# A ring of four PSUM banks for attention and feed-forward, three steps of a head pair in another place, and overwritten products of the identity ahead of P's transposes

## The chip, the cores and the metric

The kernel runs on one core of one Trainium2 chip. The metric is the device time of one execution in microseconds (us).

## The reference

```python
scores = (q @ k.transpose(0, 1, 3, 2)) / sqrt(64)      # q, k, v: 8 x 8 x 576 x 64
scores = where(pos_i // 64 >= pos_j // 64, scores, -1e9)  # causal over blocks of 64
scores = scores - max(scores)
attn = exp(scores)
attn = attn / (sum(attn) + 1e-9)
x = (attn @ v).transpose(0, 2, 1, 3).reshape(4608, 512)
h = x @ w_in                                            # 512 x 2048
g = where(h >= 1, h, where(h <= -1, 0, (h + 1) ** 2 / 4))
out = g @ w_out                                         # 2048 x 512
```

Everything is fp32, with 8 batches of 8 heads and 576 tokens of 64 values each.

## The kernel before

Attention goes by pairs of heads: 32 pairs, four to a batch. A pair's work is cut into eight steps by a generator, `attention_steps`, which yields at each step's end. The feed-forward is a second generator, `feed_forward`, with 9 chunks of 512 tokens and 16 blocks of the hidden width in each. `ffn_in` makes one block of the hidden layer with twelve products into the bank `ph` (L770), and from that `t` (L779 on ACT, L780 and L783 on DVE), `gh` (L784) and `gl` (L785). `ffn_out` multiplies `gh` and `gl` by the second weights into four banks `po` (L794, L799), twelve products again. From step 36 on (pair 4's middle) each attention step is followed by one step of the feed-forward. Pair 31 is the last, and the rest of the feed-forward runs alone behind it. In between, both weights are converted in pieces (`prepare_weights`, lines L161 to L185) up to about pair 7, some 276 us from the start.

Precision comes from splitting an operand into a high and a low part in the type fp32r, each in a product of its own; so q and k go as `qa`, `qb`, `ka`, `kb`, x as `xh` and `xl`.

One pair works like this. `turned` and `turned_last` transpose q and k on TensorE (PE) into a bank `ps_qk`, from which ACT and DVE write `qb` and `kb`; `turned_last` does it for the last block of 64 tokens. `scores(j, g)` is head j's group g of query tiles: the products L482 and L485 into a bank `ps_s`, the row maximum (L505, DVE), the exponential with its sum (L509, ACT), the sum's inverse (L491, L492) and the scaling of P (L515, DVE). `scores_last` is the last 64 queries of both heads in one go. `turn(j, g)` and `turn_last` transpose P into a bank `ps_t`; ACT copies it to `pa` or `pb` and DVE subtracts for the low part (L547). The corner, the last 64 keys of the last queries, has a transpose and a bank of its own there, and goes to `pcs`. `attn_v_first` and `attn_v(j)` multiply P by V (L591) into a bank `ps_av`, whose two halves ACT copies (L613) and DVE adds (L614) into x. `store_x` splits x.

Pairs differ by batch. In batches 0 and 1 (`plain`, pairs 0 to 7) P and V stay fp32, and P is transposed at L554; from batch 1 on P is first copied by DMA into an fp32r tile (`as_float32r`). From batch 2 on (`raw`, `far`) q and k come as fp32r from a copy in DRAM, P is transposed at L552, and each step does its turning and its P by V later than in the pairs before. For those the steps are: 0, the old pair's `turn(1, 1)`, `scores(0, 0)`, the old pair's `attn_v_first`; 1, the old pair's `turn(1, 2)`, `scores(0, 1)`, `turned_last`; 2, the old pair's `attn_v(1)` and `store_x`, `scores(0, 2)`; 3, `turn(0, 0)`, `scores_last`; 4, `turn(0, 1)`, `scores(1, 0)`, the next pair's first `turned`; 5, `turn(0, 2)`, `scores(1, 1)`; 6, `turn_last`, `scores(1, 2)`; 7, `turn(1, 0)`, `attn_v(0)`, the next pair's second `turned`.

PSUM has eight banks of 2 KB a partition. Three go round as a ring for all attention banks (`ps_w`, taken through `work_bank`), one is `ph` alone (`ps_h`), and four are `po`; until step 36 `work_bank` lends every other one of its banks from those four. A bank is written again only when its last reader is done.

Instructions are placed in each engine's queue by a scheduler of the framework, in nearly the order of the code, and each engine takes its queue in order. Tile numbers behind a name (`ps_t_8866`) count up through the program and differ between the two kernels.

Of the kernel before, what the change touches and what calls it, by code (L numbers as in the profile page):

```python
# [23 lines left out]
def block_attn_then_ffn(  # L24
# [34 lines left out]
    KA = D + NTL  # L59
    PLAIN = 2  # L60
# [13 lines left out]
    ps_w = ctx.enter_context(tc.tile_pool(name="ps_w", bufs=3, space=bass.MemoryType.PSUM))  # L74
    ps_h = ctx.enter_context(tc.tile_pool(name="ps_h", bufs=1, space=bass.MemoryType.PSUM))
# [4 lines left out]
    def work_bank(name):  # L80

# [173 lines left out]
    class Pair:  # L255
# [238 lines left out]
        def scores(self, j, g):  # L494
# [21 lines left out]
            self.pr[j, g] = as_float32r(pr[:, : cols[-1].stop], self.plain) if self.hop else [pr]  # L516

        def scores_last(self):
# [23 lines left out]
            self.pr["last"] = as_float32r(pr, self.plain) if self.hop else [pr]  # L542

        def split(self, ps, hi, lo=None):
            nc.scalar.copy(hi, ps)
            if lo is not None:
                nc.vector.tensor_tensor(out=lo, in0=ps, in1=hi.bitcast(F32), op=ALU.subtract)  # L547

# [7 lines left out]
        def turn(self, j, g):  # L556
# [15 lines left out]
        def turn_last(self):  # L572
            pr = self.pr.pop("last")
# [34 lines left out]
        def add_halves(self, ps, j, c0):  # L608
# [3 lines left out]
            xtmp = att1.tile([P, G1], F32, tag="xtmp", name="xtmp")  # L612
# [18 lines left out]
        def attn_v_first(self):  # L631
# [3 lines left out]
            for j in range(2):  # L635
                self.weighted(ps[:, j * G0 : (j + 1) * G0], j, self.parts_first(j))
            for j in range(2):
                self.add_halves(ps[:, j * G0 : (j + 1) * G0], j, 0)

        def attn_v(self, j):  # L640
# [4 lines left out]
            self.add_halves(ps, j, G0)  # L645
# [17 lines left out]
    def attention_steps():  # L663
# [10 lines left out]
        for i, cur in enumerate(pairs + [None]):  # L674
# [9 lines left out]
            if far:  # L684
                old.attn_v_first()
# [13 lines left out]
            yield  # L699
            if far:  # L700
                old.attn_v(1)
                old.store_x()
            if not cur:
                return
            if cur.far:
                cur.scores(0, 2)
# [178 lines left out]
```

## Time and profile before

| What | Value |
|---|---|
| Median of three runs | 1268.96 us (1266.4 to 1271.8) |
| Profiled execution, device time | 1269.69 us |
| Its span in the trace | 1267.9 us |
| Mean granted clock of PE | 0.981 |
| PE busy | 1200.1 us, 95% of the span, 6280 instructions |
| PE's weight loads busy | 998.8 us, 79% |
| DVE busy | 887.0 us, 70% |
| ACT busy | 703.2 us, 55% |
| POOL busy | 394.6 us, 31% |
| DMA | 215.43 MB, mean 170 GB/s |
| Chain that ended last | PE 69%, DVE 16%, ACT 6%, issue 5% |

PE is the matmul engine, DVE the vector engine, ACT the scalar engine, POOL GpSimd, SP the engine that issues most transfers. Busy shares are of the whole span. The chain is followed back from the last instruction, at each step to what released it, and its shares say on which engine the end was waiting. The granted clock is the share of TensorE's full speed that the throttle allowed. In the timeline a row has the start, the duration, the engine, the line and the operation, and in brackets the idle time ahead of it with its releaser.

### The profile page before, as it was taken

What the parts mean: (1) busy time and instruction counts of PE and PEld (TensorE: products, weight loads), DVE (VectorE), ACT (ScalarE), POOL (GpSimd) and SP (SyncE); (2) the same over time, 40 slices, a digit from 0 to 9 for tenths busy, and PEclk for the clock granted to TensorE, in tenths of its full rate; (3) what the DMA queues carried; (4) which work ended last, traced back from release to release, by engine and by line L of the source; (5) the groups of instructions that cost most, each with busy time, mean ns of one, the idle gap of its engine ahead of it and who ended that gap; (6) DMA issues with size and microseconds to landing.
All of it is one profiled execution on the core that took longest, in us unless ns stands there. A gap on an engine that the chain in (4) does not pass through costs nothing.

```text
span 1267.9 us, 20253 instructions
## 1 busy us (share of the span) xinstructions
PE 1200.1 (95%) x6280; PEld 998.8 (79%) x6280; DVE 887.0 (70%) x2188; ACT 703.2 (55%) x1827; POOL 394.6 (31%) x430
## 2 busy tenths in 40 slices
PE   5888889899999999999999999999999999999998
PEld 4666667678888888888888888888888888888886
DVE  8898877758777777777777777787777777322222
ACT  5787656646566655665656655566556555222222
POOL 3555655522222222222222222222222222222222
PEclk9888988999999999999999999999999999999999
DMA  5566666667888655555554655465556433422432
GB/s 158 167 176 215 203 228 197 217 198 237 260 273 266 215 162 158 154 175 163 156 162 145 187 157 152 138 189 153 160 154 190 137 128 118 132 87 98 133 100 100
DMA packets 185259, 215.43 MB, mean 170 GB/s; under 512 B 113840, under 2 KB 132272, under 8 KB 184384
## 3 DMA queue, kind: packets, MB, share of 16 engines
q1 hardware_dynamic: 185152, 214.14, 54.9%
q8 instruction: 50, 0.82, 0.3%
q14 instruction: 57, 0.47, 0.1%
HBM read 134.74 MB, written 31.98 MB: 131 GB/s over the span
## 4 chain that ended last, share of the span: by engine, by line
PE 69%; DVE 16%; ACT 6%; issue 5%; DMA 1%; POOL 1%; SPq 1%; ACTq 0%; POOLq 0%; DVEq 0%
PE ph L770 29%; PE po L794 15%; PE po L799 7%; PE ps_av L591 7%; PE ps_s L482 4%; ACT pr L509 3%; PE ps_s L485 3%; DVE t L780 2%; PE ps_t L552 2%; DVE t L783 2%; ACT t L779 2%; DVE pb L547 2%; DVE nm L505 2%; DVE sm L491 1%; DVE pr L515 1%
## 5 line engine op out<-in xcount | busy, mean ns | idle before, releaser
L785 POOL TENSOR_TENSOR gl<-t,gh 128x512 fp32r<-128x512 f32 x144 | 187.5, 1302 | 510.2 <-ACT gh L784 333.2
L794 PE MATMUL po<-wo,gh 128*128 128x512 f32 x1152 | 296.1, 397 | 0.5 <-DMA wo<-wo_split 0.3
L794 PEld LDWEIGHTS po<-wo,gh 128*128 128x128 f32 x1152 | 212.5, 189 | 44.5 <-DMA wo<-wo_split 0.7
L770 PE MATMUL ph<-xh,wih 128*128 128x512 f32 x576 | 232.9, 404 | 1.6 <-DVE t L783 1.6
L770 PE MATMUL ph<-xh,wil 128*128 128x512 f32 x576 | 228.8, 397 | 0.0
L770 PE MATMUL ph<-xl,wih 128*128 128x512 f32 x576 | 227.8, 396 | 0.5 <-DVE xl L627 0.5
L780 DVE SCALAR_TENSOR_TENSOR t<-t 128x512 f32<-128x512 f32 x144 | 101.5, 705 | 168.0 <-ACT t L779 165.2
L779 ACT ACTIVATE t<-ph 128x512 f32<-128x512 f32 x144 | 85.9, 597 | 173.8 <-PE ph L770 173.8
L509 ACT ACTIVATE pr<-ps_s,nm 128x128 f32<-128x128 f32 (+3 forms) x256 | 134.1, 527 | 60.5 <-DVE nm L505 58.4
L784 ACT CAST gh<-t 128x512 fp32r<-128x512 f32 x144 | 89.5, 621 | 120.3 <-DVE t L783 120.0
L799 PE MATMUL po<-wo,gl 128*128 128x512 f32 x576 | 155.6, 392 | 0.0
L482 PE MATMUL ps_s<-ka,qa 68*128 68x288 f32 (+4 forms) x384 | 135.3, 367 | 15.0 <-ACT pr L509 5.4
L379 POOL TENSOR_TENSOR vsr<-vn,vsr 128x256 fp32r<-128x256 f32 (+1 forms) x96 | 55.2, 576 | 246.2 <-ACT vsr L378 244.6
L770 PEld LDWEIGHTS ph<-xh,wil 128*128 128x128 f32 x576 | 109.5, 190 | 23.8
L770 PEld LDWEIGHTS ph<-xh,wih 128*128 128x128 f32 x576 | 109.8, 191 | 21.7 <-DVE t L783 2.3
L799 PEld LDWEIGHTS po<-wo,gl 128*128 128x128 f32 x576 | 108.7, 189 | 23.1
L505 DVE TENSOR_REDUCE nm<-ps_s 128x1 f32<-128x128 f32 (+3 forms) x256 | 118.8, 482 | 10.4 <-PE ps_s L485 9.4
L770 PEld LDWEIGHTS ph<-xl,wih 128*128 128x128 f32 x576 | 109.7, 190 | 20.5 <-DVE xl L627 0.9
L485 PE MATMUL ps_s<-kb,qb 128*128 128x288 f32 (+4 forms) x384 | 121.1, 322 | 0.0
L515 DVE TENSOR_SCALAR pr<-pr,sm 128x128 f32<-128x128 f32 (+3 forms) x256 | 107.3, 440 | 5.4
L783 DVE TENSOR_TENSOR t<-ph,t 128x512 f32<-128x512 f32 x144 | 98.7, 686 | 2.2
L491 DVE TENSOR_SCALAR sm<-sm 128x1 f32<-128x1 f32 (+1 forms) x224 | 52.0, 232 | 68.3 <-ACT pr L509 65.7
(111 smaller groups left out, 1871.4 us busy)
## 6 DMA issues: line engine op xcount, KB each, us to landing
wo<-wo_split SPq DMA_DIRECT2D x144, 512.0 KB, 3.5
prr<-pr SPq DMA_DIRECT2D x96, 192.0 KB, 2.5
prr<-pr SPq DMA_DIRECT2D x72, 256.0 KB, 2.8
out_dram<-ob SPq DMA_DIRECT2D x36, 256.0 KB, 2.9
bits<-in_moe_w_in_dram SPq DMA_DIRECT2D x32, 256.0 KB, 3.5
bits<-in_moe_w_out_dram SPq DMA_DIRECT2D x32, 256.0 KB, 3.0
wo_split<-ws SPq DMA_DIRECT2D x16, 512.0 KB, 2.9
qa<-qb SPq DMA_DIRECT2D x63, 128.0 KB, 2.4
```

The source lines that it names most:

```text
L482: nc.tensor.matmul(ps, qa[:KA, j, c0 : c0 + P], ka[:KA, j, k0 : k0 + n], start=first, stop=False)
L485: nc.tensor.matmul(ps, qb[:, j, c0 : c0 + P], kb[:, j, k0 : k0 + n], start=False, stop=last)
L505: nc.vector.tensor_reduce(out=nm[:, i : i + 1], in_=ps[:, cs], axis=AX.X, op=ALU.max, negate=True)
L509: nc.scalar.activation(pr[:, cs], ps[:, cs], AF.Exp, bias=nm[:, i : i + 1], scale=1.0, accum_out=sm[:, i : i + 1],)
L515: nc.vector.tensor_scalar_mul(pr[:, cs], pr[:, cs], sm[:, i : i + 1])
L770: nc.tensor.matmul(ph, w[:, cc, fs], x[:, cc, xs], start=(cc == 0 and i == 0), stop=(cc == NCC - 1 and i == 2),)
L779: nc.scalar.activation(t_, ph, AF.Relu, bias=0.5, scale=0.5)
L780: nc.vector.scalar_tensor_tensor(out=t_, in0=t_, scalar=1.0, in1=t_, op0=ALU.min, op1=ALU.mult)
L783: nc.vector.tensor_tensor(out=t_, in0=ph, in1=t_, op=ALU.max)
L785: nc.gpsimd.tensor_tensor(out=gl, in0=t_, in1=gh.bitcast(F32), op=ALU.subtract)
L794: nc.tensor.matmul(po[tt], gh[:, ts_], wo[:, w, :], start=(fc == 0 and w == 0), stop=False)
L799: nc.tensor.matmul(po[tt], gl[:, ts_], wo[:, 0, :], start=False, stop=fc == NFC - 1)
```

## The change

It has three parts.

The ring. `ps_h` goes, `ps_w` has four banks, and `ffn_in` takes `ph` through `work_bank` as attention takes its own. `po` keeps four.

The steps of `far` pairs. Step 0 does the old pair's `attn_v(0)` in place of `attn_v_first`, step 1 does `attn_v_first` behind `scores(0, 1)`, and step 2 does `scores(0, 2)` ahead of `attn_v(1)`. Step 7 no longer has `attn_v(0)`. `turned_last` moves from a pair's own step 1 to the end of step 6 of the pair before it. The corner is no longer transposed in step 6 into a bank of its own, but in step 7 into the free columns of `turn(1, 0)`'s bank (`turn_corner`). `add_halves` is given its scratch `xtmp` by the caller, one tile for both calls in `attn_v_first`. `moved` holds what `scores` wrote out before.

The products. In `plain` pairs `turn` and `turn_last` call `dense` ahead of their transposes: two products of the identity with itself, 512 columns each, into the bank that the transposes then overwrite. There are 7 such sets in each of 8 pairs, 112 products of 512 columns in all.

```diff
+    DENSE = 2
...
-    ps_w = ctx.enter_context(tc.tile_pool(name="ps_w", bufs=3, space=bass.MemoryType.PSUM))
-    ps_h = ctx.enter_context(tc.tile_pool(name="ps_h", bufs=1, space=bass.MemoryType.PSUM))
+    ps_w = ctx.enter_context(tc.tile_pool(name="ps_w", bufs=4, space=bass.MemoryType.PSUM))
...
+        def dense(self, ps):
+            part, cols = ident_r.ap
+            moving = bass.AP(tensor=ident_r.tensor, offset=ident_r.offset, ap=[part, [0, 4], cols])
+            for _ in range(DENSE if self.plain else 0):
+                nc.tensor.matmul(ps, ident_r, moving, start=True, stop=True)
...
             ps = work_bank("ps_t")
+            self.dense(ps)
             for c0 in range(0, n, P):
                 self.transposed(ps[:, c0 : c0 + P], pr, c0, P)
+            if self.far and j == 1 and g == 0:
+                self.turn_corner(self.pr.pop(("last",)), ps[:BLK, n : n + P])
...
         def turn_last(self):
...
+            self.dense(ps)
...
-            ps = work_bank("ps_t")
-            self.transposed(ps[:BLK, :P], pr, SM, BLK)
-            self.split(
-                ps[:BLK, :P].rearrange("p (h c) -> p h c", h=2), *(x[:BLK] for x in self.pc)
-            )
+            if not self.far:
+                self.turn_corner(pr, work_bank("ps_t")[:BLK, :P])
...
             if far:
-                old.attn_v_first()
+                old.attn_v(0)
...
                 cur.scores(0, 1)
-                cur.turned_last()
+                if not cur.raw:
+                    cur.turned_last()
...
+            if far:
+                old.attn_v_first()
...
+            cur.scores(0, 2)
             if far:
                 old.attn_v(1)
                 old.store_x()
...
+            if nxt and nxt.raw:
+                nxt.turned_last()
             yield
             if cur.far:
                 cur.turn(1, 0)
-                cur.attn_v(0)
...
-        ph = ps_h.tile([P, 512], F32, tag="ph", name="ph")
+        ph = work_bank("ph")
```

Three places show how instructions move. In these rows a line of PE holds the line of code, the bank written, the operands and, in brackets, what it waits for.

First, PE from step 5 of a far pair to step 1 of the next. Before:

```order
L485 MATMUL ps_s_8830<-kb_107,qb_105 128x384
...
L552 MATMUL ps_t_8866<-ident_r_95,prr_8740 128x128 [waits DMAHW5_49,DVE_49,PE_49]
L552 MATMUL ps_t_8873<-ident_r_95,prr_8742 64x128 [waits DMAHW6_49,DVE_49]
L482 MATMUL ps_s_8877<-ka_106,qa_104 128x512 [waits Activation_49]
L485 MATMUL ps_s_8877<-kb_107,qb_105 128x512
...
L591 MATMUL ps_av_8984<-pa00_8697,vsr0_111 128x256 [waits DVE_49,PE_49]
...
L552 MATMUL ps_t_9011<-ident_r_95,prr_8888 128x128 [waits DMAHW5_49,DVE_49]
L482 MATMUL ps_s_9018<-ka_106,qa_104 128x384 [waits Activation_49]
L485 MATMUL ps_s_9018<-kb_107,qb_105 128x384
L442 MATMUL ps_qk_9031<-ident_r_95,qk_8744 128x128 [waits DVE_49,PE_49]
```

After; the same stretch has these rows, L486 for L485, L566 for L552, L443 for L442, L611 for L591 and L795 for L770:

```order
L486 MATMUL ps_s_9321<-kb_104,qb_102 128x384
...
L566 MATMUL ps_t_9357<-ident_r_92,prr_9231 128x128 [waits DMAHW0_49,DVE_49,PE_49]
L483 MATMUL ps_s_9364<-ka_103,qa_101 128x512 [waits DVE_49]
L486 MATMUL ps_s_9364<-kb_104,qb_102 128x512
L443 MATMUL ps_qk_9377<-ident_r_92,qk_9235 128x128 [waits Activation_49]
...
L566 MATMUL ps_t_9397<-ident_r_92,prr_9289 128x128 [waits DMAHW4_49,DVE_49]
L566 MATMUL ps_t_9397<-ident_r_92,prr_9233 64x128 [waits DMAHW1_49]
L402 MATMUL ps_qk_9406<-ident_r_92,qk_9235 128x128 [waits DVE_49]
L795 MATMUL ph_9417<-xh_94,wih_96 128x512 [waits Activation_49]
...
L611 MATMUL ps_av_9468<-pb0_9192,vsr0_108 128x320 [waits DVE_49,PE_49]
```

The corner (64x128) no longer stands ahead of `scores(1, 2)` in a bank of its own, but behind `turn(1, 0)`'s transposes in theirs. `turned_last` (`ps_qk`, one row of 128 columns) stands right behind `scores(1, 2)`, and no longer behind `scores(0, 1)` of the next pair; and the feed-forward's `ph` and `attn_v(0)`'s first product now wait for ACT and DVE where they take their bank.

Second, DVE over the same steps 6 and 7. Before, whole:

```order
L547 TENSOR_TENSOR pb1_8702<-ps_t_8866,pb0_8701 128x4x2x64 [waits Activation_49]
L783 TENSOR_TENSOR t_8856<-ph_8843,t_8856 128x512 [waits DVE_49]
L547 TENSOR_TENSOR pcs1_110<-ps_t_8873,pcs0_109 64x128 [waits Activation_49]
L505 TENSOR_REDUCE nm_8879<-ps_s_8877 128x1 [waits PE_49]
L491 TENSOR_SCALAR sm_8880<-sm_8880 128x1 [waits Activation_49]
L492 RECIPROCAL sm_8880<-sm_8880 128x1 [waits DVE_49]
L515 TENSOR_SCALAR pr_8878<-pr_8878,sm_8880 128x512 [waits DMAHW6_49,DMAHW5_49,DVE_49]
L547 TENSOR_TENSOR pa11_8700<-ps_t_8902,pa10_8699 128x384 [waits Activation_49]
L614 TENSOR_TENSOR x32_8703<-ps_av_8908,xtmp_8919 64x320 [waits Activation_49,Pool_49]
L389 SCALAR_TENSOR_TENSOR qb_105<-ps_qk_8922,qb_105 64x512 [waits Activation_49]
L395 TENSOR_TENSOR kb_107<-ps_qk_8922,kb_107 64x512 [waits Activation_49]
```

After (L808 is the old L783, L506 the old L505, L390 and L396 the old L389 and L395, L554 the old L547):

```order
L808 TENSOR_TENSOR t_9347<-ph_9334,t_9347 128x512 [waits DVE_49]
L506 TENSOR_REDUCE nm_9366<-ps_s_9364 128x1 [waits PE_49]
L390 SCALAR_TENSOR_TENSOR qb_102<-ps_qk_9377,qb_102 64x2x64 [waits Activation_49]
...
L516 TENSOR_SCALAR pr_9365<-pr_9365,sm_9367 128x512 [waits DMAHW1_49,DMAHW0_49,DVE_49]
L447 TENSOR_SCALAR ka_103<-ps_qk_9377 64x2x64
L554 TENSOR_TENSOR pcs1_107<-ps_t_9397,pcs0_106 64x128 [waits Activation_49]
L390 SCALAR_TENSOR_TENSOR qb_102<-ps_qk_9406,qb_102 64x512 [waits Activation_49]
L554 TENSOR_TENSOR pa11_9191<-ps_t_9397,pa10_9190 128x384 [waits Activation_49]
L396 TENSOR_TENSOR kb_104<-ps_qk_9406,kb_104 64x512 [waits Activation_49]
```

Four small pieces of `turned_last` (64x2x64) have come in behind the row maximum of `scores(1, 2)`, the corner's subtraction (`pcs1`) has moved from ahead of that maximum to behind the scaling of P, and the add of x (L614) has left for a later step.

Third, PE in a `plain` pair, from the products of one `scores` to those of the next. Before:

```order
L482 MATMUL ps_s_934<-ka_106,qa_104 128x384 [waits Activation_49]
L485 MATMUL ps_s_934<-kb_107,qb_105 128x384
L554 MATMUL ps_t_945<-ident_r_95,pr_838 128x128 [waits DVE_49,Activation_49]
L554 MATMUL ps_t_945<-ident_r_95,pr_838 128x128
L554 MATMUL ps_t_945<-ident_r_95,pr_838 128x128 [waits Activation_49]
L554 MATMUL ps_t_945<-ident_r_95,pr_838 128x128
L554 MATMUL ps_t_951<-ident_r_95,pr_838 64x128
L422 MATMUL ps_qk_954<-ident_r_95,ks_888 128x128 [waits Pool_49]
L422 MATMUL ps_qk_954<-ident_r_95,ks_888 128x128 x3
L482 MATMUL ps_s_961<-ka_106,qa_104 128x512 [waits Activation_49]
```

After (L561 is the product of the identity, L568 the old L554):

```order
L483 MATMUL ps_s_965<-ka_103,qa_101 128x384 [waits Activation_49]
L486 MATMUL ps_s_965<-kb_104,qb_102 128x384
L561 MATMUL ps_t_976<-ident_r_92 128x512 [waits PE_49]
L561 MATMUL ps_t_976<-ident_r_92 128x512
L423 MATMUL ps_qk_987<-ident_r_92,ks_917 128x128 [waits Activation_49,Pool_49]
L423 MATMUL ps_qk_987<-ident_r_92,ks_917 128x128 x3
L561 MATMUL ps_t_1005<-ident_r_92 128x512 [waits Activation_49]
L561 MATMUL ps_t_1005<-ident_r_92 128x512
L568 MATMUL ps_t_976<-ident_r_92,pr_865 128x128 [waits DVE_49]
L568 MATMUL ps_t_976<-ident_r_92,pr_865 128x128 x3
L568 MATMUL ps_t_984<-ident_r_92,pr_865 64x128 [waits PE_49]
L483 MATMUL ps_s_994<-ka_103,qa_101 128x512
```

Each bank `ps_t` is first written by two products of 512 columns. Here both sets stand some rows ahead of their transposes; of the 56 sets 42 stand directly ahead of them.

More of the change, by code (lines that the diff above doesn't have):

```diff
@@ L699, in attention_steps @@
             yield
+            if not cur:
+                old.attn_v(1)
+                old.store_x()
+                return
+            if not cur.far:
+                cur.begin()
+            cur.scores(0, 2)
             if far:
@@ L702, in attention_steps @@
                 old.store_x()
[L703 to L706, printed above, removed]
-            else:
-                cur.begin()
-                cur.scores(0, 2)
+            if not cur.far:
                 cur.turn(0, 0)
```

22 lines of the change are left out of this document (15 added, 7 removed).

## The prediction

> **What bounds the kernel now.** I read the totals by stage first, then the clock line of the page, then the chain in the two halves of the first stage, and last, for the long second stage, what TensorE waits for.
>
> ```profile
> PEclk9888988999999999999999999999999999999999
> 0.00:276.00 276.00, 227.38 (x1107) 179.53 (x1108) 221.34 (x601) 181.63 (x526) 140.04 (x177) 0.92 0.63 196
> 276.00:1080.00 804.00, 789.88 (x4369) 668.67 (x4368) 615.80 (x1515) 477.27 (x1228) 210.60 (x220) 1.00 0.58 176
> 1080.00:1267.90 187.90, 182.79 (x807) 150.64 (x805) 49.89 (x73) 44.27 (x74) 43.99 (x34) 0.99 0.33 108
> ```
>
> Columns are the stretch, its length, busy time of PE, PE's weight loads, DVE, ACT and POOL, the granted clock, DMA share and GB/s. The middle stage, pairs 8 to 31 beside the feed-forward, is PE's: 98% busy at full clock. The tail is PE's too and the change leaves it alone. In the first stage, while weights convert, PE is busy 82% and DVE 80%, and the clock is 0.92. Nine stretches there, 44.38 us together, run at half clock; here are the third, the fourth and the sum, and how one product of 512 columns lasts before and after 32.7 us:
>
> ```profile
> 101.02:104.43 3.41, 3.41 (x8) 2.14 (x7) 3.41 (x15) 3.41 (x14) 0.11 (x2) 0.50 0.84 310
> 114.67:118.09 3.42, 3.42 (x10) 2.64 (x9) 3.28 (x8) 1.41 (x5) 1.68 (x2) 0.50 0.55 189
> sum 44.38, PE 40.46 PEld 30.42 DVE 37.72 ACT 26.17 POOL 22.08; mean PE 4.50 PEld 3.38 DVE 4.19 ACT 2.91 POOL 2.45
> L485 PE MATMUL ps_s<-kb,qb 128*128 128x512 f32 x2 | 1.3, 628 | 0.0
> L485 PE MATMUL ps_s<-kb,qb 128*128 128x512 f32 x1 | 0.4, 401 | 0.0
> ```
>
> The last two rows (windows 12.3 to 32.7 and 33 to 49.8) say that the start ran at half clock as well, though its clock column reads 1.00. What a dip costs shows in the chain that ended last, where the same work stands in a dip (first and third row) and out of it:
>
> ```profile
> 101.02 6.56 PE ps_av L591 x20
> 275.16 5.07 PE ps_av L591 x20
> 113.61 4.62 PE ph L770 x12
> 254.83 2.75 PE ph L770 x12
> ```
>
> So a dip of 3.4 us costs 1.5 to 1.9 us where PE is on the chain. It is there only in part:
>
> ```profile
> by line: PE ps_av L591 8.7%; DVE pr L515 8.2%; DVE nm L505 7.6%; DVE work L171 6.9%; PE ps_t L554 6.3%; DVE work L177 5.8%; issue 5.8%; DVE work L174 4.6%; PE ph L770 3.7%; PE ps_s L482 2.9%; DVE nm L529 2.3%; PE ps_s L485 2.1%; DMA ka<-mro
> by line: PE ph L770 15.6%; PE ps_av L591 12.7%; issue 11.5%; POOL work L183 6.7%; PE po L794 5.6%; DVE t L780 3.2%; DMA prs<-pr 3.1%; PE po L799 3.0%; ACT pr L509 2.7%; DMA bits<-in_moe_w_in_dram 2.6%; DMA kn<-in_k_dram 2.2%; DVE t L783 2.2
> ```
>
> From 0 to 145 us (first row) PE's shares add up to 24%, from 145 to 290 us to 37%. DVE carries much of the rest.
>
> The middle stage has two waits of PE that come back in each of its pairs (window 290 to 1080):
>
> ```profile
> PEld ps_qk L442 <- PE ps_s L485: 15.7, 23, 0.7
> PEld ps_s L482 <- ACT pr L509: 10.1, 23, 0.5
> 679.54 0.25 PE L442 MATMUL ps_qk<-ident_r,qk 128*128 128x128 f32 x1 [0.38 <-DVE x L614]
> 711.83 0.41 PE L482 MATMUL ps_s<-ka,qa 68*128 68x384 f32 x1
> 712.08 0.34 PE L485 MATMUL ps_s<-kb,qb 128*128 128x384 f32 x1
> 712.25 0.43 DVE L614 TENSOR_TENSOR x<-ps_av,xtmp 64x256 f32<-64x256 f32 x1
> 712.83 0.25 PE L442 MATMUL ps_qk<-ident_r,qk 128*128 128x128 f32 x1 [0.41 <-DVE x L614]
> ```
>
> First, L442 (`turned_last`) takes the bank of `attn_v_first`, whose last add (L614) ends at 712.68; PE starts at 712.83, 0.75 us after L485. The 384 columns before it need some 0.18 (an estimate from 0.23 us for 512 columns, below), so about 0.57 is lost, 23 times: 13.1 us. Second, `scores(1, 2)` waits for the exponential of `scores(1, 1)`: 10.1 us. Together 23 us of 804.
>
> **The change part by part.** The sum is made against the profiled execution, 1269.69 us with a span of 1267.9; the median of the runs shown, 1268.96, lies 0.7 below it.
>
> *Waits removed.* The corner of the last block no longer takes a bank in step 6, and `turned_last` no longer stands behind `attn_v_first`. Both waits above go: -23. That is one end of this term.
>
> *Waits added.* A step that goes to step 6 brings its work for DVE along, into a stretch where DVE is already late. The rows of one pair:
>
> ```profile
> 731.71 0.51 PE L552 MATMUL ps_t<-ident_r,prr 128*128 128x128 f32 x5
> 732.51 0.50 PE L482 MATMUL ps_s<-ka,qa 68*128 68x512 f32 x1 [0.29 <-ACT pr L509]
> 733.09 2.00 PE L794 MATMUL po<-wo,gh 128*128 128x512 f32 x8
> 735.84 0.37 PE L552 MATMUL ps_t<-ident_r,prr 128*128 128x128 f32 x3
> 734.42 0.68 DVE L783 TENSOR_TENSOR t<-ph,t 128x512 f32<-128x512 f32 x1
> 735.01 0.27 DVE L547 TENSOR_TENSOR pcs<-ps_t,pcs 64x128 fp32r<-64x128 f32 x1
> 735.21 0.67 DVE L505 TENSOR_REDUCE nm<-ps_s 128x1 f32<-128x512 f32 x1
> 735.97 0.69 ACT L509 ACTIVATE pr<-ps_s,nm 128x512 f32<-128x512 f32 x1 [0.22 <-DVE nm L505]
> 681.19 0.28 DVE L389 SCALAR_TENSOR_TENSOR qb<-ps_qk,qb 64x128 fp32r<-64x128 f32 x1
> 737.17 0.49 DVE L515 TENSOR_SCALAR pr<-pr,sm 128x512 f32<-128x512 f32 x1
> 737.57 0.55 DVE L547 TENSOR_TENSOR pa<-ps_t,pa 128x384 fp32r<-128x384 f32 x1
> 738.78 0.68 DVE L389 SCALAR_TENSOR_TENSOR qb<-ps_qk,qb 64x512 fp32r<-64x512 f32 x1 [0.21 <-ACT qb L388]
> 740.11 0.69 DVE L395 TENSOR_TENSOR kb<-ps_qk,kb 64x512 fp32r<-64x512 f32 x1 [0.65 <-ACT kb L394]
> 741.30 1.03 PE L591 MATMUL ps_av<-pa,vsr 128*128 128x256 f32 x8
> ```
>
> I lay the new order on these rows. With the wait gone, PE begins `scores(1, 2)` at 732.0; its two products take 0.58 (732.51 to 733.09), `turned_last` 0.1, the twelve products of `ffn_out` 2.75 (733.09 to 735.84), two sets of four small products 0.6. So the feed-forward's bank `ph` is wanted at 736.0. In the ring of four it is the bank of `scores(1, 2)`, which the exponential frees. The corner's subtraction (L547 of `pcs`) no longer stands ahead of the reduction, so that runs at 735.0 in place of 735.2, the exponential from 735.8 to 736.5, and PE hears of it 0.14 later (the add ended at 712.68, PE started at 712.83): 736.6. New wait: 0.55. Behind it DVE has `turned_last`'s four small pieces (0.28 each), the scaling of P (0.49), the corner (0.27), then `qb` (0.68), P's subtraction (0.55) and `kb` (0.69): 3.8 us, of which one small piece fits in before the exponential ends at 736.5, and with two tiny ones for the sum and its inverse `kb` ends near 740.3. `attn_v(0)` wants that bank 3.6 us after 736.6, at 740.2, and gets it at 740.4: 0.2. The two cost 0.75 in each of 24 pairs, 18 us, and the term is -23 + 18 = -5. It rests on DVE's queue to within some 0.6 us a pair, so it may be from -23 to +9; I take -6, near the sum, because every piece in it has a row.
>
> *The other pieces of the ring.* `ph` and the work banks share four where there were three and one. The closest case on the rows above: `ph` of step 5 is read last by L783, which ends at 735.10, and its bank is wanted by the transposes of step 7 at 735.4. That just fits, so nothing is costed; were L783 half a microsecond later, this would be a third wait. `xtmp` is taken once for two halves, but the second copy still waits for the first add; nothing. `attn_v(1)` behind `scores(0, 2)` delays the write of x by 0.5 us, and its reader comes a step later; nothing, unless that step shrinks.
>
> *The dense products.* 56 sets (7 in each of 8 pairs) of two products of 512 columns: by the row of eight `po` (2.75 us for twelve) 0.23 each at full clock, 25.8 us of PE. They hide where PE waits for P anyway:
>
> ```profile
> L554 PE MATMUL ps_t<-ident_r,pr 128*128 128x128 f32 x96 | 20.4, 339 | 14.8 <-DVE sm L491 7.5 <-DVE pr L515 3.9 <-ACT pr L535 1.6
> L552 PE MATMUL ps_t<-ident_r,vsr 128*128 128x128 f32 x65 | 8.2, 242 | 3.0 <-DMA vsr<-pr 1.4 <-ACT pr L535 1.0 <-DVE xl L627 0.6
> L552 PE MATMUL ps_t<-ident_r,pre 128*64 128x128 f32 x4 | 1.0, 260 | 3.7 <-ACT pr L509 3.0 <-ACT pb L545 0.7
> ```
>
> That is 21.5 us of waiting (up to 276 us), in gaps of up to 3.8. A set fills at most 0.46 of one, so some twenty sets hide, 9 us. Of the other 17 a third would count by PE's share of the chain, all of it if PE were the chain; I take half, +8. Ends: 0 and +25.8.
>
> *The clock.* At most half of 44.4 us, 22, and half of some 20 us at the start come back, -32, if no dip is left; none if all stay. The dips follow stretches in which PE was little busy:
>
> ```profile
> 97.61:101.02 3.41, 1.94 (x17) 1.72 (x16) 3.31 (x9) 2.76 (x8) 2.71 (x4) 1.00 0.83 257
> ```
>
> 1.94 us busy of 3.41, then half clock. Two dense sets there would make it 2.8. I take five of the nine dips as lifted, 20 us of the 44, and the start as a few us shorter: -13. With the price, -5 for this stage. The Trainium skill (TensorE: Matmul & The Clock Gate, Part 1, the table of the two states) has the clock fall after a whole idle window of about 3.4 us. The trace differs: this window was 57% busy. Taken strictly the rule leaves 0.46 us of products in a gap without any effect on the clock, and the sum would be -6 + 8.
>
> Sum: -6 - 5 = -11, so 1258.7 for the profiled execution and 1258 for the median.
>
> **The rivals.** A: PE's new waits do not come, because DVE gets through its queue 0.6 us earlier than I laid it. Then -23 - 5 = -28: 1241. For it: DVE still idles 0.65 us ahead of `kb` in the row at 740.11. Against: 3.8 us of its work stand in line behind the reduction.
>
> B: the dense products do not lift the dips. Then -6 + 8: 1271, no change. For it: a gap of 1.5 us or more is not closed by 0.46. This is what the rule of TensorE: Matmul & The Clock Gate in the Trainium skill would make of it.
>
> C: all dips go, the start's in part: -26 + 8 - 6 = -24: 1245. Against: where PE waits ahead of scores or of the feed-forward, no dense set stands.
>
> D, on the other side: the scheduler issues a dense set as soon as its bank is free, rows ahead of its transposes, while PE has work. Then nothing hides, no gap is filled, and the 25.8 us stand on the path: -6 + 25.8 = +20, 1289; with 12.5 us of them on the path it is slower by 0.5%. Against: in the order most sets stand right ahead of their transposes.
>
> **How the numbers follow.** The median's noise is about 0.5%, 6.3 us: faster is under 1262.6, slower over 1275.3. Chances: the forecast 0.42 (1251 to 1265), A 0.17, B 0.16, C 0.11, D 0.14. Below 1262.6 lie nearly all of A and C and 0.36 of the forecast: 0.63. The same: the rest of the forecast, B but for a little, and a little of D: 0.21. Slower: 0.16. The range 1242 to 1276 leaves out half of A and most of D.
>
> **What the profile after would show.** No wait of `turned_last` on `attn_v_first`, and none of `scores(1, 2)`; in their place one of `ph` on the exponential and of `ps_av` on DVE's `kb`, 0.5 and 0.2 us. A pair's period, 33.3 us now (679.54 to 712.83 at L442), about 33.1. Four dips instead of nine before 276 us, full clock before 32 us, the end of the first stage some 5 us earlier. I am wrong if the new waits are missing or over 1 us, or if the dips stay.

## The result: slower by 0.9%

| | before | changed |
|---|---|---|
| Median | 1267.29 us (1264.21 to 1271.8, 5 runs) | 1278.59 us (1275.79 to 1281.46, 5 runs) |
| Ratio | | 1.0086, 95% interval 1.0068 to 1.0104 |
| Profiled execution, span | 1267.9 us | 1274.8 us |
| Mean granted clock in the profile | 0.981 | 0.992 |

The forecast was 1258, with a range that ended at 1276. The profiled execution of the changed kernel (1276.59) is one of its quicker ones; the five go from clock 0.983 at 1281.46 us to 0.992 at 1275.79.

The totals by stage of the changed kernel, in the columns of the prediction's first totals:

```profile
0.00:276.00 276.00, 233.93 (x1209) 188.09 (x1210) 216.43 (x601) 181.56 (x521) 138.10 (x176) 0.96 0.66 202
276.00:1080.00 804.00, 789.12 (x4339) 664.58 (x4339) 619.75 (x1507) 474.61 (x1228) 210.49 (x220) 1.00 0.57 173
```

The first stage has the clock that was hoped for, 0.96 where it was 0.92, with PE busy 6.6 us longer; the middle stage shows 30 products fewer in the same 804 us. Where a pair's first product of scores starts tells how far each stage got. Pair 8's, the end of the first stage, and the last pair's `scores(1, 2)`, the end of the middle, of before:

```profile
270.46 0.22 PE L482 MATMUL ps_s<-ka,qa 68*128 68x128 f32 x1
1066.05 0.50 PE L482 MATMUL ps_s<-ka,qa 68*128 68x512 f32 x1
```

And of the changed kernel:

```profile
272.92 0.22 PE L483 MATMUL ps_s<-ka,qa 68*128 68x128 f32 x1
1072.96 0.47 PE L483 MATMUL ps_s<-ka,qa 68*128 68x512 f32 x1
```

So the first stage ends 2.5 us later, the middle takes 800.04 in place of 795.59, 4.5 us more, and what follows is the same (201.84 and 201.85 us to the span's end). What PE's weight loads wait for in the middle stage (window 290 to 1080; total, times, longest):

```profile
PEld ph L795 <- ACT pr L510: 8.9, 17, 0.5
PEld ps_qk L443 <- ACT pr L510: 7.9, 23, 0.5
PEld ps_s L483 <- PE ps_t L566: 6.3, 17, 0.4
PEld ps_av L611 <- PE ps_s L486: 4.6, 17, 0.3
```

Both waits of before (25.8 us together) are gone, and `ph` waits for the exponential and `attn_v(0)` (L611) waits, as forecast. The third row is new: `scores(0, 0)`. The second costs PE next to nothing, since at L443 the loads wait while PE is still in the products before. One pair in order of time, PE, ACT and DVE:

```profile
771.14 0.28 PE L443 MATMUL ps_qk<-ident_r,qk 128*128 128x128 f32 x1
774.41 0.69 ACT L510 ACTIVATE pr<-ps_s,nm 128x512 f32<-128x512 f32 x1
775.24 0.50 PE L795 MATMUL ph<-xh,wih 128*128 128x512 f32 x1 [0.38 <-ACT pr L510]
775.51 0.29 DVE L396 TENSOR_TENSOR kb<-ps_qk,kb 64x128 fp32r<-64x128 f32 x1
776.02 0.28 DVE L447 TENSOR_SCALAR qa<-ps_qk 64x128 fp32r<-64x128 f32 x1
776.73 0.29 DVE L447 TENSOR_SCALAR ka<-ps_qk 64x128 fp32r<-64x128 f32 x1
777.06 0.28 DVE L554 TENSOR_TENSOR pcs<-ps_t,pcs 64x128 fp32r<-64x128 f32 x1
777.37 0.48 ACT L552 CAST pa<-ps_t 128x384 fp32r<-128x384 f32 x1 [1.12 <-DVE pcs L554]
777.37 0.69 DVE L390 SCALAR_TENSOR_TENSOR qb<-ps_qk,qb 64x512 fp32r<-64x512 f32 x1
778.09 0.56 DVE L554 TENSOR_TENSOR pa<-ps_t,pa 128x384 fp32r<-128x384 f32 x1
778.10 0.38 PE L566 MATMUL ps_t<-ident_r,prr 128*128 128x128 f32 x3
778.70 0.69 DVE L396 TENSOR_TENSOR kb<-ps_qk,kb 64x512 fp32r<-64x512 f32 x1
778.75 0.30 PE L483 MATMUL ps_s<-ka,qa 68*128 68x128 f32 x1 [0.27 <-PE ps_t L566]
779.54 1.32 PE L611 MATMUL ps_av<-pb,vsr 128*128 128x320 f32 x8
804.93 0.28 PE L443 MATMUL ps_qk<-ident_r,qk 128*128 128x128 f32 x1
```

DVE reads the bank of `turn(1, 0)` last (`pa`, to 778.65), 0.1 us before `scores(0, 0)` starts in it; `kb` ends at 779.39, and `attn_v(0)` starts 0.15 later. For both the views name PE's own work as what came last (the brackets at 778.75, the last row of the list above); that DVE holds them is read from these times, and tested with f2 below. This pair takes 33.79 us (771.14 to 804.93), where the prediction's row had 33.29; over 22 pairs the mean goes from 33.43 to 33.62.

The list of waits alone doesn't give the loss: it holds 25.8 us that went and 19.8 that came (8.9, 6.3 and 4.6), yet the middle stage is 4.5 longer. So PE's lost time was counted over both traces from the start of each product to the start of the next, less 0.23 us for every 512 columns:

| Lost in the middle stage, us | before | changed | difference |
|---|---|---|---|
| `turned_last` and the other turns to `ps_qk` | 15.0 | 1.9 | -13.1 |
| `scores(1, 2)` | 8.8 | 0.8 | -8.0 |
| first product of `ph` | 1.8 | 11.6 | +9.8 |
| `scores(0, 0)` | 0.7 | 7.9 | +7.2 |
| turns to P by V (`attn_v(0)`) | 1.2 | 4.8 | +3.6 |
| `po` behind `po`, at most 0.1 us each | 2.4 | 6.8 | +4.4 |
| turns to P's transposes | 0.4 | 3.4 | +3.0 |
| all else | 46.9 | 44.1 | -2.8 |

The rows add up to +4.1 (the two traces differ by 0.4 in the columns themselves). The first five come to -0.5. The rest of the loss is in small pieces whose cause no run here singles out.

Last, the six half-clock stretches that are left in the first stage, the first of them and their sum, and three of the stretches of 3.41 us ahead of such places:

```profile
24.51:27.92 3.41, 3.02 (x12) 2.14 (x11) 3.27 (x13) 2.59 (x9) 2.19 (x3) 0.50 0.82 265
...
sum 20.49, PE 19.76 PEld 15.07 DVE 15.58 ACT 14.31 POOL 12.02; mean PE 3.29 PEld 2.51 DVE 2.60 ACT 2.38 POOL 2.00
137.15:140.56 3.41, 1.67 (x8) 0.89 (x7) 3.34 (x9) 2.57 (x6) 0.74 (x1) 1.00 0.47 120
41.58:44.99 3.41, 1.75 (x14) 1.38 (x12) 3.07 (x12) 2.43 (x8) 1.61 (x2) 1.00 0.75 184
65.47:68.88 3.41, 0.39 (x2) 0.00 (x0) 3.38 (x11) 1.19 (x4) 1.46 (x2) 1.00 0.02 5
```

20.5 us in place of 44.4, and the start is at half clock until 17.7 us in place of 32.8. The profile's clock, 0.992, is above the mean of the five, 0.989; the kernel before has 0.982 on average over the timed runs beside the experiments. Twice the missing share of the span puts the half-clock time at some 29 us in place of 45 (an estimate, with the few us at the span's end in it), so about 16 us went in an average run and not 24.

### The profile page after: what moved, and what is told of

The parts are those of the page before. It is cut to its first block, busy times and chain, and to the rows that moved or that the text cites. A ratio compares the mean times of both kernels' runs of the same rounds, so it can differ in the third digit from the quotient of the medians.

```text
span 1274.8 us, 20343 instructions
## 1 busy us (share of the span) xinstructions
PE 1212.8 (95%) x6392; PEld 1009.4 (79%) x6392; DVE 889.7 (70%) x2188; ACT 703.4 (55%) x1827; POOL 393.9 (31%) x430
## 4 chain that ended last, share of the span: by engine, by line
PE 61%; DVE 15%; ACT 5%; issue 2%; DMA 2%; POOL 0%; SPq 0%; ACTq 0%; POOLq 0%; DVEq 0%
PE ph L795 24%; PE po L819 14%; PE ps_av L611 8%; PE po L824 7%; PE ps_s L483 3%; PE ps_s L486 3%; ACT pr L510 3%; DVE pb L554 2%; DVE t L805 2%; PE ps_t L566 2%; DVE t L808 2%; DVE pr L516 2%; DVE nm L506 2%; DVE kb L396 1%; DVE sm L492 1%
## 5 line engine op out<-in xcount | busy, mean ns | idle before, releaser
L810 POOL TENSOR_TENSOR gl<-t,gh 128x512 fp32r<-128x512 f32 x144 | 191.9, 1332 | 623.1 <-ACT gh L809 216.6
L795 PE MATMUL ph<-xh,wih 128*128 128x512 f32 x576 | 232.3, 403 | 13.0 <-ACT pr L510 12.7
L819 PEld LDWEIGHTS po<-wo,gh 128*128 128x128 f32 x1152 | 208.1, 188 | 40.0 <-ACT gh L809 0.5
L795 PE MATMUL ph<-xh,wil 128*128 128x512 f32 x576 | 227.0, 394 | 0.0
L795 PE MATMUL ph<-xl,wih 128*128 128x512 f32 x576 | 226.3, 393 | 0.0
L483 PE MATMUL ps_s<-ka,qa 68*128 68x288 f32 (+4 forms) x384 | 129.3, 352 | 10.6 <-PE ps_t L566 4.4
L506 DVE TENSOR_REDUCE nm<-ps_s 128x1 f32<-128x128 f32 (+3 forms) x256 | 119.0, 482 | 28.5 <-PE ps_s L486 28.2
L795 PEld LDWEIGHTS ph<-xh,wih 128*128 128x128 f32 x576 | 109.3, 190 | 35.7 <-ACT pr L510 16.0
L795 PEld LDWEIGHTS ph<-xh,wil 128*128 128x128 f32 x576 | 109.1, 189 | 24.3
L795 PEld LDWEIGHTS ph<-xl,wih 128*128 128x128 f32 x576 | 109.5, 190 | 19.6
L486 PE MATMUL ps_s<-kb,qb 128*128 128x288 f32 (+4 forms) x384 | 119.6, 318 | 0.0
L516 DVE TENSOR_SCALAR pr<-pr,sm 128x128 f32<-128x128 f32 (+3 forms) x256 | 114.6, 468 | 4.7
L808 DVE TENSOR_TENSOR t<-ph,t 128x512 f32<-128x512 f32 x144 | 98.6, 685 | 2.3
L380 POOL TENSOR_TENSOR vsr<-vn,vsr 64x64 fp32r<-64x64 f32 (+1 forms) x96 | 50.8, 530 | 149.3 <-ACT vsr L379 142.4
L566 PEld LDWEIGHTS ps_t<-ident_r,prr 128*128 128x128 f32 x600 | 68.3, 139 | 25.8 <-issue 3.6
```

Of the source, the lines that this page charges most:

```text
L483: nc.tensor.matmul(ps, qa[:KA, j, c0 : c0 + P], ka[:KA, j, k0 : k0 + n], start=first, stop=False)
L486: nc.tensor.matmul(ps, qb[:, j, c0 : c0 + P], kb[:, j, k0 : k0 + n], start=False, stop=last)
L506: nc.vector.tensor_reduce(out=nm[:, i : i + 1], in_=ps[:, cs], axis=AX.X, op=ALU.max, negate=True)
L516: nc.vector.tensor_scalar_mul(pr[:, cs], pr[:, cs], sm[:, i : i + 1])
L795: nc.tensor.matmul(ph, w[:, cc, fs], x[:, cc, xs], start=(cc == 0 and i == 0), stop=(cc == NCC - 1 and i == 2),)
L808: nc.vector.tensor_tensor(out=t_, in0=ph, in1=t_, op=ALU.max)
```

## The experiments

The columns: median and ratio to before of timed runs with 95% interval; then, from one profile each, the end of the first stage (start of pair 8's scores), PE busy and idle up to there, half-clock time at the start and after it, and the middle stage (from there to the last pair's `scores(1, 2)`). All in us.

A column from one profile is one execution, and the clock differs between executions of one kernel. The profile of g2 has the lowest clock of its seven runs (0.976, mean 0.982), those of g4 and h4 are above the mean of theirs (0.986, mean 0.983). In e2 the mean is 0.983 as in the kernel before beside it, in g1 0.986. The runs of each letter stand beside runs of the kernel before that are their own, partly on another chip; between letters the ratios are the better comparison.

| Kernel | Median | Ratio | Stage 1 ends | PE busy / idle | Half clock | Middle |
|---|---|---|---|---|---|---|
| before | 1267.3 | 1 | 270.5 | 222.1 / 48.4 | 32.8 + 44.4 | 795.6 |
| changed | 1278.6 | 1.0086 (1.0068-1.0104) | 272.9 | 230.8 / 42.1 | 17.7 + 20.5 | 800.0 |
| e1_no_dense | 1274.8 | 1.0059 (1.0047-1.0071) | 271.5 | 217.2 / 54.2 | 30.5 + 47.8 | 799.0 |
| e2_dense_only | 1280.9 | 1.0105 (1.0092-1.0118) | 282.3 | 241.9 / 40.4 | 21.5 + 47.8 | 795.7 |
| e3_ring_only | 1268.3 | 1.0008 (0.9999-1.0017) | 271.6 | 218.3 / 53.3 | 31.2 + 47.8 | 793.5 |
| e4_steps_only | 1272.7 | 1.0038 (1.0026-1.0050) | 270.9 | 222.8 / 48.1 | 31.8 + 51.2 | 801.3 |
| f1_corner_last | 1276.2 | 1.0078 (1.0061-1.0095) | 272.4 | 218.3 / 54.1 | 31.4 + 47.8 | 801.1 |
| f2_last_on_act | 1264.4 | 0.9988 (0.9977-0.9998) | 269.5 | 216.6 / 52.9 | 29.7 + 47.8 | 791.1 |
| f3_last_back | 1270.2 | 1.0038 (1.0022-1.0055) | 269.3 | 216.4 / 52.9 | 29.6 + 47.8 | 795.9 |
| f4_dense_b0 | 1277.9 | 1.0090 (1.0074-1.0106) | 273.1 | 226.2 / 46.9 | 16.7 + 44.4 | 800.3 |
| g1_dense_b0_ph | 1266.4 | 0.9982 (0.9967-0.9996) | 267.8 | 230.8 / 37.0 | 20.0 + 34.1 | 795.9 |
| g2_dense_b0_old | 1273.2 | 1.0038 (1.0024-1.0052) | 276.9 | 235.2 / 41.7 | 19.2 + 58.0 | 795.7 |
| g3_act_dense | 1266.4 | 0.9990 (0.9977-1.0003) | 272.7 | 230.8 / 41.9 | 17.6 + 20.5 | 790.1 |
| g4_dense_one | 1271.1 | 1.0028 (1.0016-1.0040) | 265.2 | 224.2 / 41.0 | 18.7 + 34.1 | 801.6 |
| h1_before_act | 1268.1 | 1.0003 (0.9989-1.0016) | 266.7 | 219.3 / 47.3 | 31.4 + 41.0 | 796.5 |
| h2_old_banks_act | 1267.0 | 0.9991 (0.9976-1.0005) | 266.9 | 217.8 / 49.1 | 31.1 + 37.5 | 795.5 |
| h3_old_act_ph | 1265.8 | 0.9984 (0.9970-0.9998) | 264.1 | 226.0 / 38.1 | 11.0 + 30.7 | 794.4 |
| h4_act_dense_one | 1261.0 | 0.9944 (0.9924-0.9965) | 265.7 | 225.1 / 40.6 | 18.6 + 34.1 | 790.6 |

**The three parts one by one.** e1 is the change without its products (`DENSE = 0`).

> The changed kernel without the products of the identity (DENSE = 0), ring and steps as changed. Theory R (the feed-forward's bank in the ring costs: in pairs 4 to 7, where ph waited 5.8 us for exponentials, and 0.2 us in each later pair): the loss stays and the clock's gain of 3 us at the start goes, so 1278 to 1284, end of the first stage 5 us later than before or more, pair period 33.6 to 33.8 us on average. Theory D (the 26 us of dense products are what the first stage lost in pairs 4 to 7): 1270 to 1274, first stage as before, middle stage 5 us longer than before. In both the half-clock time before 280 us goes back up from 38 to about 75 us.

e2 is the kernel before with `dense` and its two calls, e3 that with the ring alone, e4 the changed steps with the old banks and no products:

```diff
# e3, from before; e4 is the reverse, from e1
-    ps_w = ... bufs=3 ...
-    ps_h = ... bufs=1 ...
+    ps_w = ... bufs=4 ...
-        ph = ps_h.tile([P, 512], F32, tag="ph", name="ph")
+        ph = work_bank("ph")
```

> The kernel before with the dense products alone; ring of three, bank of its own for ph, steps as before. Theory R: the clock's gain without the ring's loss, so 1260 to 1265, middle stage the same as before (33.43 us a pair). Theory D: the dense products cost more than the clock returns, 1270 to 1276, lost in pairs 4 to 7 again.

> The kernel before with the ring of four that ph shares, and nothing else. Theory R: ph waits for exponentials in the order of before as well, first stage 5 us or more later than before and the middle stage longer, 1275 to 1285. Theory S (the steps of the far pairs, which bring DVE 0.9 us of turned_last's pieces and the corner at its busiest, make the middle stage's loss, not the ring): middle stage no longer than before, 1262 to 1270.

> The changed steps with the old banks (ring of three, ph alone), no dense products. Theory R: first stage as before (the steps touch far pairs alone), ph no longer waits, but the transposes of q and k in step 7 take the bank of scores(1, 2) in the ring of three: 0.4 to 1 us in each pair, 1275 to 1290. Theory S: the same waits on DVE as in the changed kernel, scores(0, 0) 0.4 and attn_v(0) 0.3 us a pair, so 33.7 us a pair, 1272 to 1276.

Theory R falls: the ring alone changes nothing measurable (1.0008), and its middle stage is even 2.1 us shorter (the wait of `turned_last` only moves to `ph` there, 13.4 us in its list). The steps make the middle 5.7 us longer, and with the ring it is 3.4; so the middle stage's loss is the steps'. Of the waits that each theory expected in e4, all came:

```profile
PEld ps_qk L403 <- ACT pr L511: 12.7, 17, 0.8
PEld ps_av L612 <- PE ps_s L487: 5.0, 18, 0.3
PEld ps_s L484 <- PE ps_t L567: 4.7, 18, 0.3
```

Theory D is right in its sign, but its 1270 to 1274 for e1 was just too low, and on the kernel before the products cost far more (13 us) than on the changed one (1278.6 less 1274.8). Nor did the first stage of e1 end 5 us late, as theory R had it (271.5 against 270.5).

**The middle stage.** f1 and f2 and f3 all start from e1. f1 splits P ahead of the corner:

```diff
-            if self.far and j == 1 and g == 0:
-                self.turn_corner(self.pr.pop(("last",)), ps[:BLK, n : n + P])
+            corner = self.far and j == 1 and g == 0
+            if corner:
+                self.transposed(ps[:BLK, n : n + P], self.pr.pop(("last",)), SM, BLK)
             if g == 0:
                 self.split(ps[:, :n], *self.pa[j])
+                if corner:
+                    self.split(ps[:BLK, n : n + P] ..., *(x[:BLK] for x in self.pc))
```

> Changed ring and steps without the dense products, and in turn(1, 0) P's own split comes first and the corner's behind it, out of the same bank. Theory K (ACT's copy of P stands 1.1 us behind DVE's read of the corner, because both read one bank and are taken one after the other; that holds the bank that scores(0, 0) takes and kb behind it): the waits of scores(0, 0), 0.45 us a pair, and attn_v(0), 0.26, go for the most part, 33.1 to 33.4 us a pair where it was 33.77, 1262 to 1269. Theory Q (DVE's queue is too long with turned_last's four pieces, in whatever order): the bank comes free no earlier, 33.7 us a pair, 1273 to 1276.

K came from the row at 777.37, where ACT sat idle for 1.12 us until DVE had read the corner. Its range was missed: 1276.2, with the wait of `scores(0, 0)` as it was, that of `attn_v(0)` (L617 here) at 8.2 us where e1 has 4.9, and ACT's wait now at the corner (waits in f1, 290 to 1080):

```profile
PEld ps_av L617 <- PE ps_s L486: 8.2, 18, 0.9
PEld ps_s L483 <- PE ps_t L566: 6.4, 17, 0.4
ACT pcs L552 <- DVE pa L554: 21.2, 18, 1.2
```

In the changed kernel it was at `pa`:

```profile
ACT pa L552 <- DVE pcs L554: 25.0, 24, 1.1
```

The two reads of one bank follow one another either way, and the bank is free when the second is done. So f1 doesn't take the handover away; that it isn't what costs is seen in the pair shown above. ACT's copy is done at 777.85, and DVE, with hardly a gap between its rows from 776.73 to 779.39, doesn't reach `pa` before 778.09. The Trainium skill (PSUM — Partial Sum Buffer, PSUM bank collisions raise a hardware error) has every two engines on one bank kept apart, two readers too; by that rule there is a handover in either order, and the trace agrees (25.0 and 21.2 us of ACT's waiting).

f2 takes two of `turned_last`'s four pieces from DVE to ACT, f3 puts `turned_last` back into step 1:

```diff
-                    nc.vector.tensor_scalar_mul(
+                    nc.scalar.mul(
                         last_blocks(a)[:D], ps[i * D : (i + 1) * D], 1.0 if i else SCALE
```

> Changed ring and steps without the dense products, and two of turned_last's four pieces (qa and ka, 0.28 us each) on ACT in place of DVE. Theory Q: DVE gets 0.57 us earlier to the bank of scores(0, 0) and to kb, both waits all but gone, 33.2 us a pair, 1264 to 1268. Theory K: ACT's copy of P still waits for the corner, which DVE reaches 0.3 to 0.6 us earlier, but ACT has the 0.56 us ahead of that copy now; 33.5 to 33.8 us a pair, 1270 to 1275.

> Changed ring and steps without the dense products, and turned_last back in a pair's own step 1, behind scores(0, 1). Theory Q: all four pieces, 1.1 us, are off DVE's queue there, the waits of scores(0, 0) and attn_v(0) gone, ph's wait of 0.57 stays or goes to another bank: 33.0 to 33.3 us a pair, 1260 to 1267. Theory K: ACT's copy of P still stands behind the corner, now earlier by the pieces that went; part of the waits stays, 33.3 to 33.6, 1266 to 1272.

f2 gives theory Q's numbers: 1264.4, some 9 us below e1 by the ratios (10 by the medians), the middle 7.9 shorter. Both waits are off the list, with `ph`'s left of the three, and a pair takes 33.14 us (two rows of L443). One pair of this profile has a half-clock stretch of 3.41 us in it and takes 36.4, so without that the middle would be some 3 us shorter still. The wait in f2, 290 to 1080, and three rows in order of time:

```profile
PEld ph L795 <- ACT pr L510: 8.4, 16, 0.5
627.69 0.28 PE L443 MATMUL ps_qk<-ident_r,qk 128*128 128x128 f32 x1
660.83 0.28 PE L443 MATMUL ps_qk<-ident_r,qk 128*128 128x128 f32 x1
766.25 0.56 DVE L554 TENSOR_TENSOR pa<-ps_t,pa 128x384 fp32r<-128x384 f32 x1
```

In the last row, a later pair, `pa` ends at 766.81, 2.77 us behind the start of that pair's `ph` at 764.04; in the changed kernel that was 3.41 (775.24 to 778.65), so 0.57 us of DVE work moved has bought 0.64. ACT's wait for the corner went with it (0.3 us in f2), but in the pair above it had cost DVE nothing. f3 missed Q's range by 3 us and lies in K's: the waits of `scores(0, 0)` are nearly off the list (0.6 us), but `ph` now waits in all 23 pairs and `attn_v(0)` as before:

```profile
PEld ph L792 <- ACT pr L510: 11.9, 23, 0.5
PEld ps_av L611 <- PE ps_s L486: 4.4, 16, 0.3
PEld ps_s L483 <- PE ps_t L566: 0.6, 2, 0.4
```

In a pair of f3 DVE still works without a pause from the exponential's end to that of `kb` (769.79 to 772.87), and `attn_v(0)` starts 0.15 later. The queue is shorter there, 3.1 us, and still holds PE; theory Q had it gone.

Two controls. h1 is f2's edit on the kernel before, h2 the same on e4.

> The kernel before with turned_last's qa and ka on ACT, nothing else. Theory Q (DVE's queue is late only where the change put turned_last, behind scores(1, 2)): in step 1 DVE is not what PE waits for, so 1265 to 1269, the same. Rival (the edit gains wherever it stands, and the changed steps are a loss by themselves): 1256 to 1262.

> The changed steps with the old banks (1272.7 us as they stood) and turned_last's qa and ka on ACT, no dense products. Theory Q: the waits of scores(0, 0), 0.34, and attn_v(0), 0.26, go, the one of the transposes of q and k on the exponential of scores(1, 2), 0.66, stays: 33.2 us a pair, 1262 to 1266, so the ring is not needed for it. Rival (the gain needs the ring's fourth bank): 1268 to 1273.

h1: the same as before (1.0003), so the edit is worth nothing where DVE isn't what PE waits for. h2: 5.7 us below e4, the middle as long as before's; `attn_v(0)` still waits there (4.6 us), and with the ring the middle is another 4.4 shorter (791.1 against 795.5). For the whole kernel the two ratios, 0.9988 and 0.9991, don't tell f2 from h2. So h2 missed its range by 1 us, and the rival that the gain needs the ring is right for a part at most.

**The dense products.** f4 keeps them for pairs 0 to 3 (`self.b == 0`) in the changed kernel, g2 in the kernel before. g1 is g2 with another bank for them, the feed-forward's, which stands idle until step 36; there they hardly wait, and the scheduler puts many of them further ahead and several sets in a row. g4 is the changed kernel with `DENSE = 1`.

```diff
# g1
+            ps = ps_h.tile([P, 512], F32, tag="ph", name="dn")
             for _ in range(DENSE):
                 nc.tensor.matmul(ps, ident_r, moving, start=True, stop=True)
```

> The changed kernel with the dense products in pairs 0 to 3 alone, half of them. Theory D (their price is paid in pairs 4 to 7, where PE has the feed-forward to do, and the clock's gain is made in pairs 0 to 3, where PE waits): 1271 to 1274, below the 1274.8 without any, pair 4 starting at 98 to 99 us. Rival (what is gained up to pair 4 is lost again by pair 8, because the weights' conversion and not PE sets when the first stage ends): 1274 to 1276, the same as without any.

> The kernel before with dense products for pairs 0 to 3 alone, 28 sets, written to the feed-forward's bank ph, which stands idle there, so that none waits for a bank and the scheduler puts them where its plan has PE idle. Theory W (dense products on the old ring cost 13 us because they wait for their bank ahead of the transposes, 11.7 us in all, and then run behind the gap that they should have filled): no such wait, the clock's dips before 98 us mostly gone, 1261 to 1268. Theory P (their 13 us of PE time are paid wherever they stand): 1272 to 1278, pair 4 starting 5 us later than before.

> The kernel before with the dense products of pairs 0 to 3 alone, in the transposes' own banks of the old ring. Theory W: waits for banks ahead of the products as with all 56 sets, pair 4 starting 5 to 7 us late and 1271 to 1277. Theory P: half of the 13.4 us that all 56 cost, 1272 to 1275, and within 2 us of the same products in the bank ph.

> The changed kernel with one dense product a set in place of two, 12.9 us of PE in place of 25.8. Theory price (PE time on the path against clock returned in the same measure): between 1274.8 without any and 1278.6 with two, 1275 to 1278. Rival (one product is too little to hold the clock, so that its price stands without a return): 1279 to 1283, half-clock time before 280 us near 75 us as without any.

f4 fits neither theory: half of the products cost as much as all (1277.9). In its profile two half-clock stretches of 6.8 us fall into pair 4, behind the last of them. g1 and g2 have the same 56 products; in the bank of the transposes they cost 5.5 us, in the idle bank they gain 1.3, as theory W has it. The totals up to the end of the first stage, in g2 (before had 270.46 us with PE busy 222.1):

```profile
0.00:276.92 276.92, 235.18 (x1136) 185.98 (x1137) 219.54 (x593) 179.08 (x512) 134.57 (x173) 0.90 0.62 192
```

And in g1:

```profile
0.00:267.81 267.81, 230.80 (x1137) 177.92 (x1137) 217.83 (x593) 177.96 (x511) 136.44 (x172) 0.94 0.64 198
```

g2: PE busy 13.1 us longer, about what 56 products take at full clock (0.23 each), idle 6.7 shorter. g1: busy 8.7 longer, since more of it ran at full clock, idle 11.4 shorter. The profile of g2 is its slowest run (1276.27), so the two profiles lie 9 us apart where the medians differ by 6.8. Where PE waited, up to 290 us, stands behind the second bar as the idle time ahead of a group. In e2, the products (L555) and P's transposes (L562):

```profile
L555 PE MATMUL ps_t<-ident_r 128*128 128x512 f32 x112 | 41.5, 454 | 5.3 <-ACT pr L510 3.8 <-DVE qa L430 1.5
L562 PE MATMUL ps_t<-ident_r,pr 128*128 128x128 f32 x96 | 18.7, 319 | 5.5 <-DVE pr L516 5.3 <-DVE sm L492 0.2
```

In g1, the products in the idle bank:

```profile
L558 PE MATMUL dn<-ident_r 128*128 128x512 f32 x56 | 25.6, 522 | 1.1
```

In the changed kernel, products (L561) and transposes (L568):

```profile
L561 PE MATMUL ps_t<-ident_r 128*128 128x512 f32 x112 | 38.8, 428 | 2.7 <-DVE qa L430 1.9 <-ACT qb L428 0.8
L568 PE MATMUL ps_t<-ident_r,pr 128*128 128x128 f32 x96 | 16.5, 286 | 11.7 <-DVE pr L516 9.6 <-DVE pr L547 2.0
```

With the old banks PE waits 3.8 us for exponentials ahead of the products themselves, and stands there with the gap unfilled; with the ring it waits 2.7 us there and 11.7 ahead of the transposes, behind the products; in the idle bank 1.1. g4 went against the rival and past the theory: 1271.1, below the kernel without any. One product takes 13.2 us off PE's idle time (54.2 to 41.0) at 7.0 more busy; two take 12.1 off at 13.6. The second fills nothing in these profiles, and the medians, 1271.1 with one and 1274.8 without, have the same order.

**Together.** g3 is the change with f2's edit, h4 that with one product, h3 is h2 with g1's products.

> The whole change, dense products included, with turned_last's qa and ka on ACT. If its parts add up: 1264.4 without dense products and the 3.8 us that they cost on the changed ring and steps, 1267 to 1271, the middle stage at 33.3 us a pair. Rival (the dense products' cost came with the late middle stage): 1263 to 1266.

> The same with the dense products of pairs 0 to 3 in the idle bank ph. If both gains add: 1.3 us below the kernel with old banks and the edit on ACT, 1260 to 1265. If the first stage's gain is lost where the stages meet: the same as that kernel within 1 us.

> The whole change with one dense product a set and turned_last's qa and ka on ACT. If both add: 1271.1 less the 10.4 that the edit brought without dense products and 12.2 with two, 1259 to 1262, below both kernels. If the one product's gain was where the middle stage's waits now are not: 1263 to 1267.

h4 adds up and is the best of all: 1260.95 us (1259.4 to 1263.44), ratio 0.9944 (0.9924 to 0.9965), the middle 790.6 and the first stage 265.7. g3 lies between its two ranges: 2.0 us above f2 by the medians, the same by the ratios (0.9990 and 0.9988), so that the price of two products vanished with the late middle stage isn't ruled out. h3 is 1.2 below h2, a microsecond past its range, and the intervals of the two overlap. The change as a whole was two edits from a gain.

## Why the prediction was wrong

*Waits removed: right.* Both are gone from the list, 25.8 us of the loads' waiting; counted from start to start, 21.1 us of PE went, where 23 were forecast.

*Waits added: the step that failed.* Of the two new waits that were laid by hand, `ph` (0.55 forecast, 0.52 a time measured) and `attn_v(0)` (0.2, measured 0.27), both came, from the rows named. A third was left out: the bank one place earlier in the ring, `turn(1, 0)`'s, which `scores(0, 0)` takes and which hangs on the same DVE queue, one piece ahead of `kb`; 0.37 a time in the list, and 7.2 us of PE in all. And the queue behind the exponential was put at 3.8 us; in the pair shown it is 4.3 (775.10 to 779.39). The term was -6 with ends -23 and +9; the middle stage measured +4.5, within the ends and on the other side of zero. The waits removed gave 21.1 us of PE and the two that were laid took 13.4, which alone would have made -7.7. The wait left out took 7.2 of that back; some 5 us more in small pieces, most of them between products of `po` and ahead of P's transposes, were not forecast either, and their cause stays open. f2 shows the hold of DVE's queue: 0.57 us off it takes 8 us out of the middle, and h1 that it counts only behind `scores(1, 2)`. Rival A had named that slack, 0.6 us a pair, as what decides; in that pair it came out 0.5 us the other way.

*The other pieces of the ring: right for the ring by itself.* Nothing was costed, and e3 measures none. My own theory R after the result blamed it, and fell. The third wait that this term feared was at another bank of the ring.

*The clock: right in its size.* 24 of 44 us of dips went in the profile, about 16 in an average run, and 15 at the start; forecast were 20 and a few. Between the profiles of e1 and the changed kernel PE's busy time grew by 13.6 us where the products take 25.8, so the clock gave 12.2 back; forecast 13. The changed kernel's profile has more clock than its average run, so 12.2 is on the high side.

*The dense products: mis-sized.* PE's idle time fell by 12.1 us (54.2 to 42.1). The forecast hid 9 and let only half of the rest count, by PE's share of the chain of waits, so 17.8 us were to cost nothing. A stage is PE's busy and idle time, so its end moves by 25.8 - 12.1 - 12.2 = 1.5 us from e1 to the changed kernel. The forecast for price and clock together was -5; the profiles give +1.5, the medians, at the lower clock of an average run, +3.8. A share of the chain says how much of a stage waited for PE as it was; that work put onto PE makes it wait more is the likely reason, and no run tests it alone.

*Rivals.* D's mechanism (products standing ahead of PE's work with nothing hidden) didn't come on the changed kernel, but something near it on the old banks. B's, that the dips stay, is what e2 shows: 47.8 us of dips with all the products, on the old ring, and the mean clock of the kernel before. For the rule in the Trainium skill that stood beside B (TensorE: Matmul & The Clock Gate, Part 1), the stretch at 137.15 is a second case against: 49% busy, never idle as a whole, half clock behind it. Yet the one at 41.58 with 51% had full clock behind it. So PE's busy share of one such stretch doesn't settle it either, and the runs leave open what does.

## What to carry to other kernels

When steps are moved in a ring of buffers, list every buffer that the late engine frees, in the ring's order, with its next taker; the one that was left out here was the largest single part of the error. Check the sum of the listed waits against the time of the stage as well: here the list said 6 us less and the stage took 4.5 more. An engine that is busy 70% over all can be the bound for four microseconds in each round, and half a microsecond a round moved off it there was worth 8 us over the stage, and nothing elsewhere. Filler products pay for as long as there is a gap to fill: one a set did, the second only took time, and where they had to wait for their bank they stood behind the gap.

## What was not expected

The same filler products lifted the half-clock stretches on one ring (47.8 to 20.5 us) and not on the other (44.4 to 47.8). g1 against g2 suggests that the bank they wait for has to do with it (34.1 and 58.0 us in the profiles; a mean clock of 0.986 and 0.982), but g1 also moved them in PE's queue, so the two are not told apart. f4, where half of the products left 44.4 us of dips and cost what all cost, is not explained.
